# An attention-plus-FFN kernel: weight-block differences moved from GpSimd to VectorE, and a flag set earlier

## The chip, the cores and the metric

The kernel runs on one core of one Trainium2 chip. The metric is the device time of one execution in microseconds (us); every time of a run below is such a time, and the "span" is the somewhat shorter stretch that the profiler covers. The engines of a core are TensorE (PE: matmuls; PEld: its weight loads), VectorE (DVE), ScalarE (ACT), GpSimd (POOL) and SyncE (SP, which here only issues transfers). In the traces below each works through its own queue of instructions in order, and waits where an operand or a buffer is not ready. Tiles lie in one of two memories of the core: PSUM, where every matmul of this kernel writes its result (the pools whose names begin with `ps_`), and SBUF, which holds the rest. Most executions of one kernel agree within about 1%.

## The reference

```python
def _attn_ref(q, k, v):                      # q, k, v: [8, 8, 576, 64] (batch, heads, tokens, 64)
    scores = scale * np.matmul(q, k.transpose(0, 1, 3, 2))
    mask = np.abs(pos[:, None] - pos[None, :]) <= 32          # a window of 32 to each side
    scores = np.where(mask, scores, -1000000000.0)
    ...                                                      # softmax
    return np.matmul(attn, v)

def _moe_ref(x, w_gate, w_val, w_out):       # x: [4608, 512], w_gate, w_val: [512, 1536], w_out: [1536, 512]
    g = x @ w_gate
    silu = g * (1.0 / (1.0 + np.exp(-g)))
    return silu * (x @ w_val) @ w_out
```

## The kernel before

The 4608 tokens go through the FFN in nine chunks of 512. FFN1 of a chunk has twelve blocks. In each, TensorE makes two sums of four matmuls of 128x512 (gate and value) in a PSUM tile `gv`; ScalarE applies SiLU to the first; VectorE multiplies the two into `hT`. The pool `ps_a` holds two such tiles, so block u + 2 can't start before VectorE has finished the product of block u. The attention of later tokens is woven in between.

```python
def ffn1_unit(j, fk):                        # one FFN1 block of chunk j
    gv = ps_a.tile([128, 2, 512], FP32, ...)
    for i, w in enumerate((wg16, wv16)):
        for g in range(GS):                  # GS = 4
            nc.tensor.matmul(out=gv[:, i, :], lhsT=w[:, g, ...], rhs=xts[j][:, g, :], ...)
    nc.scalar.activation(out=ssb, in_=gv[:, 0, :], func=AF.Silu, ...)
    nc.vector.tensor_tensor(out=hts[j][:, fk, :], in0=ssb, in1=gv[:, 1, :], op=ALU.mult)
```

From the second chunk on, FFN2 is computed with seven half-size products in place of eight (Winograd's form of Strassen's scheme). That takes, once, four differences T1 to T4 of blocks of `w_out`, and, for each chunk, four sums S1 to S4 of blocks of `hT`, which VectorE makes during FFN1. GpSimd makes the differences, after it has issued the loads of the third batch:

```python
    turn_x([4, 5, 6], ps_a, cast_act)
    ffn2_sub(0, 3, 0)
    pair_av(7)
    pair_mask(8)                             # VectorE: p = p * mask, 128x1024 f16, both in SBUF
    ffn2_sub(0, 3, 1)
    turn_x([7], ps_a, cast_dve)              # TensorE transposes x, VectorE copies them from PSUM into xT
    load_v(2, range(5))
    wino_weights()
    ...                                      # then FFN1 of the second chunk, which reads xT

def wino_weights():
    ...
    sub = lambda o, a, b: nc.gpsimd.tensor_tensor(out=o, in0=a, in1=b, op=ALU.subtract)
    sub(t3, b22, b12)                        # 128x1536
    sub(wide, b12, b11)                      # wide is f32, the others f16
    cast_pool(t1, wide)
    sub(wide, b22, wide)
    cast_pool(t2, wide)
    sub(t4, b21, wide)
```

At the end a flag says whether all softmax sums were in a safe range (otherwise a general path runs). One small matmul counts the partitions that passed, and VectorE turns the count into the flag. The count lies in `ps_c`, a pool of one buffer, which the first product (`p1`) of the last FFN2 also needs:

```python
def set_flag(good):
    cnt = ps_c.tile([1, 1], FP32, tag="c", name="cnt")
    nc.tensor.matmul(out=cnt, lhsT=good, rhs=ones, ...)
    nc.vector.tensor_scalar(out=flag, in0=cnt, scalar1=127.5, op0=ALU.is_lt, ...)

for j in range(1, NCH):                      # NCH = 9
    ffn1(j)
    if j == NCH - 2:
        good = check_range()                 # five small VectorE instructions
    if j == NCH - 1:
        set_flag(good)
    ffn2(j, ...)                             # p1, p2, p6, p5, p7, p3, p4: 12 matmuls of 128x256 each
```

## Time and profile before

| what | before |
|---|---|
| time, median (first three runs) | 339.58 us (337.96 to 339.7) |
| span of the profiled run | 338.0 us |
| TensorE busy | 316.1 us, 94% |
| wait for xT before the second FFN1 (gap 1) | 5.26 us |
| wait for the flag before the last FFN2 (gap 2) | 2.01 us |

From the page of the kernel before: the span; busy time, share and count of TensorE and VectorE; then two rows in which the span is cut into 40 equal slices, PE with its busy share in tenths and PEclk with the granted TensorE clock in tenths of full speed.

```profile
span 338.0 us, 7194 instructions
...
PE 316.1 (94%) x2888; PEld 183.7 (54%) x2888; DVE 206.9 (61%) x412; ACT 161.9 (48%) x245; POOL 121.9 (36%) x145
...
PE   6789999499999999999999999999999999899791
...
PEclk9999999699999999999999999999999999999987
```

TensorE is the limit. Its row has 9 nearly everywhere, and two dents: a 4 in the eighth slice (59 to 68 us) and a 7 near the end. At the first the clock falls in the same slice, at the second in the slice after it. The view of waits says what TensorE waited for (the columns are total, times, longest):

```profile
PE gv_ps L421 <- DVE xT L265: 5.3, 1, 5.3
...
PE x_ps L504 <- DVE flag L577: 2.0, 1, 2.0
...
PE x_ps L504 <- DVE s_top L476: 0.9, 1, 0.9
```

The timeline shows the first gap. Its columns are the start, the duration, engine, line and operation, out<-in, and in brackets the idle time before. L462 is the subtraction on GpSimd, L316 the mask multiply, L408 the transposes, L265 the xT copy, L421 the FFN1 matmuls.

```profile
56.98 3.12 POOL L462 TENSOR_TENSOR w_top<-wo 128x1536 f16<-128x1536 f16 x1
...
58.10 5.60 DVE L316 TENSOR_TENSOR p_t<-p_t,mask 128x1024 f16<-128x1024 f16 x1
...
58.45 0.39 PE L408 MATMUL xt_ps<-ident,x 128*128 128x128 f16 x4
...
60.03 3.12 POOL L462 TENSOR_TENSOR w_wide<-wo 128x1536 f32<-128x1536 f16 x1
...
63.21 1.82 POOL L268 CAST w_top<-w_wide 128x1536 f16<-128x1536 f32 x1
63.63 0.41 DVE L265 COPY xT<-xt_ps 128x512 f16<-128x512 f16 x1
...
64.10 1.89 PE L421 MATMUL gv_ps<-xT,wg 128*128 128x512 f16 x4 [5.26 <-DVE xT L265]
...
65.78 1.91 PE L421 MATMUL gv_ps<-xT,wv 128*128 128x512 f16 x4
...
67.48 1.31 PE L421 MATMUL gv_ps<-xT,wg 128*128 128x512 f16 x4
```

The xT copy is not slow. It stands in VectorE's queue behind a multiply that took 5.60 us, eight times its usual 0.69, exactly while GpSimd subtracted. After the gap, groups of four matmuls follow each other every 1.7 us instead of every 0.865 us.

The same view at the end of the kernel before. L576 is the count, L428 the last FFN1 product, L577 the flag, L504 the FFN2 products.

```profile
317.55 0.19 PE L576 MATMUL cnt<-ones,good 128*1 128x1 f32 x2
...
318.28 0.69 DVE L428 TENSOR_TENSOR hT<-ssb,gv_ps 128x512 f16<-128x512 f16 x1 [0.24 <-ACT ssb L427]
...
319.56 0.14 DVE L577 TENSOR_SCALAR flag<-cnt 1x1 int32<-1x1 f32 x1
...
319.75 1.91 PE L504 MATMUL x_ps<-wo,hT 128*128 128x256 f16 x12 [2.01 <-DVE flag L577]
...
321.45 2.74 PE L504 MATMUL y_ps<-wo,hT 128*128 128x256 f16 x12
```

The count is done at once, but the flag waits in VectorE's queue for the last FFN1 product and two sums. Meanwhile it holds the PSUM buffer that the first FFN2 product wants.

### The profile page before, as it was taken

How to read it: one execution, taken by the hardware profiler on the slowest of the kernel's cores; microseconds unless marked ns; L12 is line 12 of the kernel's file. 1: busy time of each engine (PE TensorE's matmuls, PEld its weight loads, DVE VectorE, ACT ScalarE, POOL GpSimd, SP SyncE). 2: the span in 40 equal slices, each digit the busy share in tenths (PEclk: the TensorE clock that was granted, in tenths of full speed). 3: DMA queues.
4: the chain of work that ended last, by engine and by line, in shares of the span. 5: the costliest groups of instructions: out<-in, count | busy, mean ns of one | idle time of the engine just before them, and what ended most of it. 6: DMA issues, size and time to landing. Idle time of an engine off the chain costs nothing. (4 is left out here: it accounts for less than half of the span.)

```text
span 338.0 us, 7194 instructions
## 1 busy us (share of the span) xinstructions
PE 316.1 (94%) x2888; PEld 183.7 (54%) x2888; DVE 206.9 (61%) x412; ACT 161.9 (48%) x245; POOL 121.9 (36%) x145
## 2 busy tenths in 40 slices
PE   6789999499999999999999999999999999899791
PEld 3444555144774477447744764486448644754380
DVE  2743375545766786778667767686668556535720
ACT  3864579057753376237533753375337633233220
POOL 8972878993704540356045405360000000000000
PEclk9999999699999999999999999999999999999987
DMA  7999999939949995999999979996531510020003
GB/s 271 171 204 303 216 162 200 152 41 136 114 119 142 156 111 117 121 162 86 192 128 133 118 166 109 151 134 150 109 49 33 142 31 3 31 93 3 0 33 100
DMA packets 154280, 41.31 MB, mean 122 GB/s; under 512 B 137856, under 2 KB 151680, under 8 KB 154240
## 3 DMA queue, kind: packets, MB, share of 16 engines
q0 software_dynamic: 100640, 16.52, 67.5%
q1 hardware_dynamic: 53600, 24.26, 31.5%
q8 instruction: 24, 0.39, 0.5%
q14 instruction: 16, 0.13, 0.1%
HBM read 37.75 MB, written 9.44 MB: 140 GB/s over the span
## 5 line engine op out<-in xcount | busy, mean ns | idle before, releaser
L428 DVE TENSOR_TENSOR hT<-ssb,gv_ps 128x512 f16<-128x512 f16 x108 | 74.3, 688 | 88.9 <-ACT ssb L427 88.9
L427 ACT ACTIVATE ssb<-gv_ps 128x512 f16<-128x512 f32 x108 | 64.5, 597 | 126.2 <-PE gv_ps L421 125.0
L421 PE MATMUL gv_ps<-xT,wg 128*128 128x512 f16 x432 | 112.1, 382 | 5.9 <-DVE xT L265 5.3
L421 PE MATMUL gv_ps<-xT,wv 128*128 128x512 f16 x432 | 111.8, 381 | 0.0
L421 PEld LDWEIGHTS <-wg 128*128 128x128 f16 x432 | 41.7, 98 | 53.8 <-DVE xT L265 5.4
L421 PEld LDWEIGHTS <-wv 128*128 128x128 f16 x432 | 42.5, 98 | 51.6 <-issue 1.1
L223 POOL DMA_DIRECT2D tok<-in_q_dram x30 | 25.4, 848 | 66.1 <-DMA qT<-tok 61.1
L312 ACT ACTIVATE p_t<-s_ps 128x1024 f16<-128x1024 f32 (+1 forms) x40 | 34.7, 924 | 13.1 <-PE s_ps L306 13.1
L504 PEld LDWEIGHTS <-hT 128*128 128x128 f16 x288 | 28.3, 100 | 7.6 <-issue 2.0
L223 POOL DMA_DIRECT2D tok<-in_k_dram x30 | 25.3, 845 | 16.3 <-DMA kT<-tok 12.2
L504 PEld LDWEIGHTS <-s_top 128*128 128x128 f16 x288 | 27.7, 98 | 4.8 <-DVE s_top L476 1.1
L316 DVE TENSOR_TENSOR p_t<-p_t,mask 128x1024 f16<-128x1024 f16 x32 | 25.9, 841 | 1.6 <-ACT p_t L312 0.9
L386 DVE TENSOR_TENSOR x<-o_ps,rall 128x512 f16<-128x512 f32 (+1 forms) x39 | 25.4, 650 | 1.3
L504 PE MATMUL x_ps<-w_top,s_top 128*128 128x256 f16 x192 | 23.8, 273 | 0.9 <-DVE s_top L476 0.9
L242 POOL DMA_DIRECT2D v<-in_v_dram x24 | 21.4, 904 | 0.4 <-DMA tok<-in_q_dram 0.4
L476 DVE TENSOR_TENSOR s_top<-hT 128x768 f16<-128x768 f16 (+2 forms) x48 | 20.1, 418 | 0.0
L265 DVE COPY v<-v 64x512 f16<-64x512 f16 x46 | 14.8, 321 | 1.6
L688 ACT ACT_TABLE_LOAD x12 | 15.4, 1283 | 0.2
L532 DVE TENSOR_TENSOR osb<-y_ps,kept 128x512 f32<-128x512 f32 (+1 forms) x16 | 10.5, 655 | 7.8 <-ACT p_t L312 4.0
L368 PEld LDWEIGHTS <-p_t 128*64 128x64 f16 x576 | 10.7, 110 | 6.9 <-issue 5.1
L262 ACT ACTIVATE kept<-x_ps 128x512 f32<-128x512 f32 (+1 forms) x18 | 9.4, 532 | 10.4 <-PE x_ps L504 10.4
L504 PE MATMUL x_ps<-wo,hT 128*128 128x256 f16 x96 | 12.2, 279 | 2.0 <-DVE flag L577 2.0
(81 smaller groups left out, 276.6 us busy)
## 6 DMA issues: line engine op xcount, KB each, us to landing
out_dram<-osb SPq DMA_DIRECT2D x32, 256.0 KB, 2.5
v<-in_v_dram POOLq DMA_DIRECT2D x24, 128.0 KB, 4.8
tok<-in_q_dram POOLq DMA_DIRECT2D x24, 128.0 KB, 4.7
tok<-in_k_dram POOLq DMA_DIRECT2D x24, 128.0 KB, 5.3
qk_st<-in_q_dram SPq DMA_DIRECT2D x4, 576.0 KB, 7.2
qk_st<-in_k_dram SPq DMA_DIRECT2D x4, 576.0 KB, 9.0
v<-in_v_dram POOLq DMA_DIRECT2D x16, 96.0 KB, 5.3
wo<-in_moe_w_out_dram POOLq DMA_DIRECT2D x4, 384.0 KB, 21.4
```

Of the source, the lines that this page charges most:

```text
L223: nc.gpsimd.dma_start(out=t[0:n].rearrange("p (h d) -> p h d", d=D), in_=src[b].rearrange("h s d -> s h d")[128 * m:128 * m + n])
L242: nc.gpsimd.dma_start(out=dst[:, 2 * m, :, 0:D], in_=src[128 * m - 32:128 * m + 96])
L265: nc.vector.tensor_copy(out=o, in_=i)
L312: nc.scalar.activation(out=o, in_=s, func=AF.Exp, bias=0.0, scale=1.0 / float(D) ** 0.5)
L316: nc.vector.tensor_tensor(out=flat, in0=flat, in1=mask, op=ALU.mult)
L386: nc.vector.tensor_tensor(out=x16s[m][:, a], in0=ov[:, :, :, 0:D], in1=r.unsqueeze(3).to_broadcast([128, a.stop - a.start, 4, D]), op=ALU. ...
L421: nc.tensor.matmul(out=gv[:, i, :], lhsT=w[:, g, 128 * fk:128 * fk + 128], rhs=xts[j][:, g, :], start=(g == 0), stop=(g == GS - 1))
L427: nc.scalar.activation(out=ssb, in_=gv[:, 0, :], func=AF.Silu, bias=0.0, scale=1.0)
L428: nc.vector.tensor_tensor(out=hts[j][:, fk, :], in0=ssb, in1=gv[:, 1, :], op=ALU.mult)
L476: tt = lambda o, a, b, op: nc.vector.tensor_tensor(out=o, in0=a, in1=b, op=op)
L504: nc.tensor.matmul(out=dst[n], lhsT=lhs[:, f, 128 * n:128 * n + 128], rhs=rhs[:, f, :], start=(first and f == 0 and (split or n == 0)), st ...
L688: nc.scalar.activation(out=dummy, in_=rall[0:1, 0, 0:1], func=func, bias=0.0, scale=1.0)
```

## The change

The intent is to take the weight differences off GpSimd, where they are slow, and to spread them in eight pieces over VectorE's idle time in the second FFN1. The second part sets the flag inside the last FFN1, where nobody waits for its buffer.

```diff
 def wino_weights():
-        wide = qkst.tile([128, FKS // 2, 256], FP32, tag="qkst", name="w_wide")
 ...
-        sub = lambda o, a, b: nc.gpsimd.tensor_tensor(out=o, in0=a, in1=b, op=ALU.subtract)
-        sub(t3, b22, b12)
-        sub(wide, b12, b11)
-        cast_pool(t1, wide)
-        sub(wide, b22, wide)
-        cast_pool(t2, wide)
-        sub(t4, b21, wide)
+        return [lambda o=o[:, f:f + 3], a=a[:, f:f + 3], b=b[:, f:f + 3]:
+                nc.vector.tensor_tensor(out=o, in0=a, in1=b, op=ALU.subtract)
+                for o, a, b in ((t3, b22, b12), (t1, b12, b11), (t2, b22, t1), (t4, b21, t2))
+                for f in (0, 3)]
 ...
-    wino_weights()
+    tw = wino_weights()
 ...                                          # in ffn1(j), after block u
+            if j == 1:
+                for f in {0: tw[0:1], 1: tw[1:3], 3: tw[3:5], 4: tw[5:7], 5: tw[7:8]}.get(u, ()):
+                    f()
+            if j == NCH - 1 and u == 4:
+                set_flag(good)
 ...
-        if j == NCH - 1:
-            set_flag(good)
```

## The prediction

> **What bounds the kernel now.** TensorE. The page has PE busy 94% of the span of 338.0 us (VectorE 61%, ScalarE 48%, GpSimd 36%). So the change is worth what it removes from TensorE's gaps. The timeline shows two large ones, and the change aims at both.
>
> **Gap 1, before the second FFN1 (58.84 to 64.10 us).** The view of waits has one wait of 5.26 us of PE gv_ps for VectorE's xT copy. That copy took 0.41 us, but stood behind one mask multiply (128x1024 f16, both inputs in SBUF) that took 5.60 us, against 0.69 us for its neighbours. It ran from 58.10 to 63.70, while GpSimd ran two subtractions of weight blocks back to back (56.98 to 60.10, 60.03 to 63.15). The Trainium skill, "SBUF — State Buffer", section "Who interferes with whom", says that a VectorE instruction with two SBUF inputs contends with a GpSimd instruction that reads SBUF and blocks; the trace agrees (5.60 against 0.69 us, ending 0.55 us after the second subtraction). After the gap the first FFN1 matmuls ran at half rate: the first three groups of four took 1.68, 1.70 and 1.14 us from start to start instead of 0.865 (granted clock 0.69 in that stretch).
>
> Without the GpSimd work (15.9 us, 56.98 to 72.8) the multiply should take 0.69 us and the xT copy start when its transposes end (58.84), so the matmuls start at about 59.4: 4.7 us gained. A gap of 0.5 us should not lower the clock: another 1.9 us.
>
> **Gap 2, before the last FFN2 (317.6 to 319.75 us).** 2.0 us of PE x_ps waiting for the flag (0.14 us on VectorE, in order behind the last FFN1 product, which ends at 318.97, and two sums). The first FFN2 product doesn't need the last FFN1 block; it waited only because the flag's count holds its PSUM buffer. With the flag at the fifth block it starts at once: 2.0 us gained. The 24 matmuls after the gap took 1.91 + 2.54 us instead of 1.31 each (granted clock 0.85): 1.8 us gained if TensorE does not pause. The second product needs the last block just when it starts: perhaps 0.1 us of wait.
>
> **What is added.** Eight f16 subtractions of 128x768 on VectorE, in the second FFN1. The sums of that shape take 0.55 us (0.47 from start to start): 4 us in all. VectorE there has 0.8 to 1.3 us idle before each FFN1 product; two pieces and a product need 1.55 us of the 1.73 us per block. I expect 0 to 0.4 us of TensorE gaps. GpSimd issues the next q, k loads some 10 us earlier; no TensorE wait for a load shows, so that gains nothing.
>
> **Sum.** 4.7 + 1.9 + 2.0 + 1.8 - 0.2 = about 10.2 us, all on TensorE's chain, which is full between the gaps, so little should be given back. 339.6 - 10.2 = 329.4 us. Range 327.5 to 332. Faster by over 2%: 0.93; within 2%: 0.06; slower: 0.01.
>
> **What would show it.** No mask multiply over 0.8 us near 58 us; gv_ps waiting about 0.5 us for xT; full-rate matmuls from the first of the second FFN1; pieces of 0.55 us; no PE wait for the flag; last FFN2 in 7 x 1.31 us.
>
> **What would make it wrong.** Clock lowered all the same, by phase or load rather than by gaps (up to 3.7 us lost); the pieces holding back FFN1 products, so that PSUM buffers come free late; earlier loads delaying transposes that FFN1 or attention need; a new wait in the last FFN2, where sums were ready early only because TensorE stood still.

## The result, and the profile after

The changed kernel takes 329.42 us (median of 4 runs, 328.64 to 330.21) against 339.64 us before. The ratio is 0.9704, 95% interval 0.9668 to 0.974: faster. Ratios below are the mean time of one kernel's fast executions over that of the other's in the same rounds, without the execution that was profiled, so they are not quite the ratio of the medians quoted. The result is correct.

From the page of the changed kernel, the same lines:

```profile
span 326.6 us, 7197 instructions
...
PE 312.4 (96%) x2888; PEld 182.3 (56%) x2888; DVE 205.9 (63%) x420; ACT 161.8 (50%) x245; POOL 106.1 (33%) x139
...
PE   6789999999999999999999999999999999899992
...
PEclk9999999999999999999999999999999999999998
```

Both dents are gone, and the clock row has no dip left before the tail. (The 8 that stays in the PE row is the wait of 0.9 us for sums, which e9_tighter below takes up.) VectorE's busy time even fell by 1.0 us, although it took on eight instructions: the time in which the multiply was blocked had been counted as busy.

The timeline of the changed kernel at gap 1 (L462 is now the piece on VectorE):

```profile
57.84 0.68 DVE L316 TENSOR_TENSOR p_t<-p_t,mask 128x1024 f16<-128x1024 f16 x1
58.18 0.39 PE L408 MATMUL xt_ps<-ident,x 128*128 128x128 f16 x4
...
58.61 0.42 DVE L265 COPY xT<-xt_ps 128x512 f16<-128x512 f16 x1
...
59.09 1.04 PE L421 MATMUL gv_ps<-xT,wg 128*128 128x512 f16 x4 [0.52 <-DVE xT L265]
...
59.97 1.03 PE L421 MATMUL gv_ps<-xT,wv 128*128 128x512 f16 x4
...
62.26 0.55 DVE L462 TENSOR_TENSOR w_top<-wo 128x768 f16<-128x768 f16 x1
...
63.99 1.02 DVE L462 TENSOR_TENSOR w_top<-wo 128x768 f16<-128x768 f16 x2
```

The multiply takes 0.68 us, TensorE waits 0.52 us, and the matmuls run at full rate from the first. Two pieces take 1.02 us and fit between two FFN1 products.

The timeline of the changed kernel at gap 2 (the count is now L572, the FFN2 products L500):

```profile
298.67 0.19 PE L572 MATMUL cnt<-ones,good 128*1 128x1 f32 x2
...
310.88 1.47 PE L500 MATMUL x_ps<-wo,hT 128*128 128x256 f16 x12
...
311.71 0.69 DVE L428 TENSOR_TENSOR hT<-ssb,gv_ps 128x512 f16<-128x512 f16 x1 [0.24 <-ACT ssb L427]
312.19 1.47 PE L500 MATMUL y_ps<-wo,hT 128*128 128x256 f16 x12
...
313.50 1.47 PE L500 MATMUL x_ps<-w_top,s_top 128*128 128x256 f16 x12
```

There is no idle time in brackets any more, and the products follow each other every 1.31 us.

For the bookkeeping, one stage measure serves for all runs below: from the end of the transposes for xT (start plus duration of that L408 line) to the first FFN2 matmul of that chunk. It was 87.33 - 58.84 = 28.49 us before and is 80.39 - 58.57 = 21.82 us after: 6.67 us gained. At the end, from the start of the last group of FFN1 matmuls to the start of the last FFN2 product, it was 329.27 - 316.59 = 12.68 us and is 318.75 - 310.02 = 8.73 us: 3.95 us gained. Against this, the stretch between the two measures is 0.37 us longer (229.63 us against 229.26), of which 0.12 us is the count, now paid inside FFN1; the other 0.25 us was not traced, and in the profiles of e1 and e2 that stretch is longer still (229.96 and 229.81 us). The rest of the profiles' 11.4 us of difference in span is scatter at both ends. The stretch before the transposes was 0.27 us shorter in this execution, and the tail after ScalarE's last copies started was 6.35 us against 7.22 (in a second profile of the changed kernel it is 6.7).

### The profile page after: what moved, and what is told of

Its sections match the earlier page's. It is cut to its first block, busy times and chain, and to the rows that moved or that the text cites. A ratio compares the mean times of both kernels' runs of the same rounds, so it can differ in the third digit from the quotient of the medians.

```text
span 326.6 us, 7197 instructions
## 1 busy us (share of the span) xinstructions
PE 312.4 (96%) x2888; PEld 182.3 (56%) x2888; DVE 205.9 (63%) x420; ACT 161.8 (50%) x245; POOL 106.1 (33%) x139
## 5 line engine op out<-in xcount | busy, mean ns | idle before, releaser
L421 PE MATMUL gv_ps<-xT,wg 128*128 128x512 f16 x432 | 110.9, 379 | 1.2 <-ACT xT L262 0.7
L500 PEld LDWEIGHTS <-hT 128*128 128x128 f16 x288 | 27.6, 98 | 5.1
L500 PEld LDWEIGHTS <-s_top 128*128 128x128 f16 x288 | 27.6, 98 | 4.7 <-DVE s_top L472 1.1
L500 PE MATMUL x_ps<-w_top,s_top 128*128 128x256 f16 x192 | 23.8, 273 | 0.9 <-DVE s_top L472 0.9
L316 DVE TENSOR_TENSOR p_t<-p_t,mask 128x1024 f16<-128x1024 f16 x32 | 20.8, 686 | 1.4 <-ACT p_t L312 0.8
L368 PE MATMUL o_ps<-v,p_t 128*64 128x66 f16 x576 | 12.8, 196 | 1.1 <-DVE p_t L352 1.1
```

Source lines behind the costliest of these rows:

```text
L316: nc.vector.tensor_tensor(out=flat, in0=flat, in1=mask, op=ALU.mult)
L368: nc.tensor.matmul(out=o[h // 4][64 * i:64 * i + 64, 66 * (h % 4):66 * (h % 4) + 66], lhsT=p[:, place(b, h)[0], i, place(b, h)[1], :], rhs ...
L421: nc.tensor.matmul(out=gv[:, i, :], lhsT=w[:, g, 128 * fk:128 * fk + 128], rhs=xts[j][:, g, :], start=(g == 0), stop=(g == GS - 1))
L500: nc.tensor.matmul(out=dst[n], lhsT=lhs[:, f, 128 * n:128 * n + 128], rhs=rhs[:, f, :], start=(first and f == 0 and (split or n == 0)), st ...
```

## The experiments

Eleven kernels ran. The theory: GpSimd's subtractions read SBUF and thereby block the mask multiply, which has both inputs in SBUF; TensorE's pause that follows also lowers its clock. Rivals are named with each run.

### Each part alone

e1_flag_only is the kernel before with only the flag moved; e2_weights_only is the changed kernel with the flag put back.

```diff
# e1_flag_only, against before
+            if j == NCH - 1 and u == 4:
+                set_flag(good)
...
-        if j == NCH - 1:
-            set_flag(good)
# e2_weights_only, against the changed kernel: the same lines the other way round
```

> The kernel before with only the flag moved into the last FFN1. If the two parts of the change are independent and gap 2 costs its 2.0 us of wait plus 1.8 us at a lowered clock: 3.7 to 3.9 us faster than before (ratio about 0.989), gap 1 unchanged at about 5.3 us. Rival, that gap 2 was hidden by the output DMA at the end or comes back as a wait for the sums: 0 to 2 us faster (ratio 0.994 to 1).

> The changed kernel with the flag put back after the last FFN1. If independent: 6.3 to 6.8 us faster than before (ratio about 0.981), gap 2 unchanged at 2.0 us with two slow products after it. Rival, that the gain of gap 1 is partly given back by the VectorE pieces or by loads issued earlier: under 5.5 us.

Measured: e1_flag_only 335.61 us against 339.44 (ratio 0.9884, interval 0.985 to 0.9919), so about 3.9 us, with the wait of gap 1 still there (5.31 us). e2_weights_only 334.43 us (ratio 0.9832, 0.9781 to 0.9883), about 5.7 us, a little under what was expected. Its stage measure is 21.81 us, the same as with the whole change, so the gain of gap 1 is not given back. The profile shows one thing that blurs the total: in this execution the very first FFN1, at 21 us, long before anything that was changed, lost about 1.7 us at half rate. Of the other profiles only e8_lump's shows that. The two parts add up to 9.6 us, against 10.0 us together (1 - 0.9704 of 339.6): they are independent within the scatter.

### Is it a lock, and on what?

e4_mask_late keeps GpSimd's work and only swaps two instructions on VectorE.

```diff
-    pair_mask(8)
     ffn2_sub(0, 3, 1)
     turn_x([7], ps_a, cast_dve)
+    pair_mask(8)
```

> The kernel before, GpSimd work kept, but the mask multiply of the eighth pair is issued on VectorE after the xT copy instead of ahead of it. Theory, GpSimd's reads block a VectorE instruction with two SBUF inputs and nothing else: the xT copy (PSUM source) still takes 0.41 us and FFN1 starts at about 59.4; the multiply still lasts till about 63.7, so the first FFN1 product comes at 63.7 instead of 61.7 and TensorE waits about 1.6 us for a PSUM buffer two blocks later, without a drop of the clock: 4 to 5 us faster than before. Rival A, VectorE as a whole is slow while GpSimd works: the copy is slow too and little is gained. Rival B, the multiply was slow for a reason of its own at that place (data or PSUM), not for GpSimd: it takes 0.69 us here and all 6.6 us are gained.

The timeline of e4_mask_late:

```profile
58.53 0.42 DVE L265 COPY xT<-xt_ps 128x512 f16<-128x512 f16 x1 [0.68 <-PE xt_ps L408]
58.87 4.47 DVE L316 TENSOR_TENSOR p_t<-p_t,mask 128x1024 f16<-128x1024 f16 x1
...
63.26 1.27 DVE L428 TENSOR_TENSOR hT<-ssb,gv_ps 128x512 f16<-128x512 f16 x2
...
63.99 1.02 PE L421 MATMUL gv_ps<-xT,wg 128*128 128x512 f16 x4 [1.35 <-DVE hT L428]
```

The copy, whose source is PSUM, takes its usual 0.42 us although GpSimd is subtracting (56.61 to 62.78 in this run), so rival A falls. The multiply is blocked again, for 4.47 us, at another place, so rival B falls. The FFN1 products, with one input in SBUF and one in PSUM, keep their 0.69 us while GpSimd goes on working. TensorE waits 1.35 us for a PSUM buffer, and its clock doesn't drop. The time is 333.56 us (ratio 0.9839, 0.9798 to 0.988), about 5.5 us faster, somewhat more than the 4 to 5 expected; the stage measure is 23.32 us, 5.17 us gained. A swap of two lines brings most of what moving all the work brings at gap 1.

e6_pool_writes keeps GpSimd busy but lets it only write. Its output is wrong, which doesn't matter for the time.

```diff
-        sub(t3, b22, b12)   ...and the other subtractions and casts
+        for t in (t3, wide, t1, t2, t4, wide, t3, wide, t1, t2, t4, wide):
+            nc.gpsimd.memset(t, 0.0)
```

> The kernel before with GpSimd's subtractions and casts replaced by twelve memsets that only write (results wrong on purpose: the differences are zero). If it is GpSimd's SBUF reads that block the mask multiply: it takes 0.69 us though GpSimd is busy beside it, and gap 1 goes, 6.3 to 6.8 us faster than before. Rival, any GpSimd access to SBUF blocks it: the multiply stays as long as the memsets that it meets, and gap 1 stays in part or whole.

The timeline of e6_pool_writes:

```profile
57.79 1.42 POOL L463 MEMSET w_wide<- 128x1536 f32 x1
57.96 0.68 DVE L316 TENSOR_TENSOR p_t<-p_t,mask 128x1024 f16<-128x1024 f16 x1
...
59.11 2.74 POOL L463 MEMSET w_top<- 128x1536 f16 x2
```

The multiply lies wholly inside a stretch of memsets without a pause and takes 0.68 us. The stage measure is 21.81 us, the same as with the change: 6.68 us gained. That points to GpSimd's reading. A memset is also another kind of instruction than a subtraction, but the traces hold a third kind: near 13 us, in all thirteen profiles, GpSimd copies two pieces of `v` from SBUF to SBUF while VectorE does mask multiplies of the same shape. From the kernel before (L352 is a multiply, L268 a copy):

```profile
12.98 0.61 POOL L268 COPY v<-v 64x512 f16<-64x512 f16 x1
13.19 0.94 DVE L352 TENSOR_TENSOR p_t<-p_t,mask 128x1024 f16<-128x1024 f16 x1
13.64 0.97 POOL L268 COPY v<-v 64x512 f16<-64x512 f16 x1
14.06 1.09 DVE L352 TENSOR_TENSOR p_t<-p_t,mask 128x1024 f16<-128x1024 f16 x1
```

The multiplies take 0.94 and 1.09 us instead of 0.69 (the slower one 1.09 to 1.10 us in every profile), and the second copy, which meets the first multiply, 0.97 us instead of 0.61. So two kinds that read SBUF, subtraction and copy, block, and the one that only writes does not. The whole time was 332.12 us against 340.06 (ratio 0.9757, 0.97 to 0.9813), nominally 8.3 us; the expected 6.3 to 6.8 lie at the edge of that interval, and in that batch the kernel before scattered from 338.57 to 341.89.

### How long does the lock hold?

In the kernel before the multiply arrived during one subtraction and waited through the next one too. e5_pool_pieces cuts GpSimd's work into eight pieces, back to back.

```diff
-        sub(t3, b22, b12)   ...and the other subtractions and casts
+        for o, a, b in ((t3, b22, b12), (t1, b12, b11), (t2, b22, t1), (t4, b21, t2)):
+            for f in (0, 3):
+                nc.gpsimd.tensor_tensor(out=o[:, f:f + 3], in0=a[:, f:f + 3],
+                                        in1=b[:, f:f + 3], op=ALU.subtract)
```

> The kernel before with the differences still on GpSimd, but as eight f16 subtractions of 128x768 back to back (about 1.6 us each, 12.5 us in all). If the lock goes back at the end of each GpSimd instruction, the mask multiply waits for at most one piece: it lasts at most 2.3 us, and 3 to 6 us are gained. If back-to-back GpSimd instructions keep VectorE out (the multiply of before waited through two of them), it lasts till GpSimd pauses, up to 12 us, and the kernel is 3 to 7 us slower than before.

The timeline of e5_pool_pieces:

```profile
56.36 6.44 POOL L464 TENSOR_TENSOR w_top<-wo 128x768 f16<-128x768 f16 x4
...
57.81 11.88 DVE L316 TENSOR_TENSOR p_t<-p_t,mask 128x1024 f16<-128x1024 f16 x1
...
62.73 3.23 POOL L464 TENSOR_TENSOR w_top<-wo,w_top 128x768 f16<-128x768 f16 x2
65.91 3.21 POOL L464 TENSOR_TENSOR ws_rest<-wo,w_top 128x768 f16<-128x768 f16 x2
```

Less GpSimd work in smaller pieces made it worse. The multiply lasted 11.88 us: through the rest of the first piece and all seven others, to 0.57 us after the last one ended. The kernel took 347.64 us (ratio 1.0258). So the end of an instruction alone does not let the waiting VectorE in. The pieces' own time per piece is 1.59 us from start to start ((62.73 - 56.36) / 4). The Trainium skill, "Perfetto Trace Analysis", section "GPSIMD Engine Instruction", advises to time GpSimd so and not by the reported spans; here the two agree (6.44 / 4 = 1.61).

What lets VectorE in? In the kernel before it came in just where GpSimd's cast had to wait for the subtraction ahead of it, whose result it read; that cast then took 1.82 us, the other one 1.46. e10_pool_chain has the same eight pieces, in an order in which a piece often has to wait for the one just ahead.

```diff
+        three = [(t1, b12, b11), (t2, b22, t1), (t4, b21, t2)]
+        for f, (o, a, b) in ([(0, x) for x in three] + [(3, x) for x in three]
+                             + [(0, (t3, b22, b12)), (3, (t3, b22, b12))]):
+            nc.gpsimd.tensor_tensor(...)      # pieces as above
```

> The GpSimd pieces of 128x768 as in the run with pieces, same number and size, but in an order in which the second and third each read what the one just ahead wrote, so that GpSimd pauses between them. There the mask multiply waited 11.2 us through seven pieces that followed each other without a pause; in the kernel before it came in where a cast had to wait for the subtraction ahead. If VectorE comes in at GpSimd's first pause: the multiply lasts at most 2.3 us, gap 1 is at most 2.2 us, 4.5 to 6.6 us faster than before. Rival, subtraction after subtraction keeps VectorE out, pause or not (in the kernel before it was the cast, another kind of instruction, that let it in): the multiply lasts 5 us or more, no gain or slower.

The timeline of e10_pool_chain:

```profile
57.71 1.65 POOL L465 TENSOR_TENSOR w_top<-wo 128x768 f16<-128x768 f16 x1
57.99 1.93 DVE L316 TENSOR_TENSOR p_t<-p_t,mask 128x1024 f16<-128x1024 f16 x1
...
59.44 1.97 POOL L465 TENSOR_TENSOR w_top<-wo,w_top 128x768 f16<-128x768 f16 x1
...
60.31 1.04 PE L421 MATMUL gv_ps<-xT,wg 128*128 128x512 f16 x4 [1.59 <-DVE xT L265]
```

Order alone cuts the multiply from 11.88 to 1.93 us. The first piece ends at 59.36; the second starts 0.08 us later, and in that pause VectorE comes in. Now the second piece pays, with 1.97 us instead of 1.64. That the pause is what lets VectorE in fits every case on record, but each order of GpSimd's work was run once; between the two copies near 13 us, which don't read each other's results, there is also a pause (0.05 us), and VectorE came in there too. The kernel took 333.68 us (ratio 0.9832, 0.9787 to 0.9877), about 5.7 us faster than before with all the work still on GpSimd; the stage measure is 22.88 us.

### Does a pause of TensorE lower its clock?

e3_fill_gap1 and e7_fill_gap2 put matmuls that nobody reads into the two gaps of the kernel before.

```diff
# e3_fill_gap1
     turn_x([7], ps_a, cast_dve)
+    idle_mms(23)
# e7_fill_gap2
             set_flag(good)
+            idle_mms(9)
```

> The kernel before with 23 matmuls of 128x512 that nobody reads put on TensorE where it waits 5.3 us for the xT copy. If the half rate after gap 1 comes from TensorE standing still: FFN1 still starts at about 64.1 but at full rate from its first matmul, 1.9 us faster than before. Rival, the clock drops there by phase or load, whatever TensorE does: no gain, still half rate.

> The kernel before with 9 matmuls of 128x512 that nobody reads in gap 2. If the slow products after gap 2 come from TensorE standing still 2 us: the last FFN2 takes 7 x 1.31 us, 1.8 us faster than before, the wait for the flag itself stays. Rival, clock by phase or load: no gain.

The timeline of TensorE in e3_fill_gap1 (L557 is the filling):

```profile
58.57 5.13 PE L557 MATMUL warm<-mask 128*128 128x512 f16 x23
63.73 1.04 PE L421 MATMUL gv_ps<-xT,wg 128*128 128x512 f16 x4
```

The multiply was still blocked (5.33 us), but the FFN1 matmuls ran at full rate at once. The stage measure is 26.29 us against 28.49. Of the 2.2 us, 1.93 come after the gap: from the first FFN1 matmul to FFN2 it is 85.03 - 63.73 = 21.30 us against 23.23. In e7_fill_gap2 the first two FFN2 products came 1.31 us apart each, instead of 1.70 and 2.56, 1.64 us gained. One profile each would be thin, but the other profiles agree: the second FFN1 started at half rate in all four with a pause of 5.3 us or more before it, and in none of the nine with a shorter one or a filled gap; the last FFN2 started at full rate in all six without a pause in gap 2 (after, e1, e8, e9, e11 and the filled e7). So the half rate came from TensorE standing still. The times of the whole kernels can't show it: the medians of the fast executions, 337.47 us (ratio 0.9926, 0.9825 to 1.0027) and 338.12 us (0.9948, 0.9872 to 1.0024) against 340.06, are inconclusive.

The profiles also add a limit to this. Seven of them have gap 2 unfilled, 2.0 us each time. The clock was lowered after it in five (before, e2, e3, e5, e6) and not in two (e4, e10). From the TensorE timeline of e10_pool_chain:

```profile
314.41 1.47 PE L502 MATMUL x_ps<-wo,hT 128*128 128x256 f16 x12 [2.02 <-DVE flag L575]
```

These 12 matmuls took 1.47 us, not 1.91, after the same pause. Single pauses before or in the second FFN1 of 1.59 (e10), 1.35 (e4) and 1.82 us (e8, next) did not lower it; the 5.3 us of gap 1 where it stayed empty (before, e1, e7) and the 11.5 us of e5 always did. The Trainium skill, "TensorE: Matmul & The Clock Gate", section "What's actually happening", says that the array runs at full or at half rate, judged over free-running windows of 3.4 us. That agrees with half rate here, and with a 2 us pause that costs something in some executions only; the windows themselves no run here shows. The half rate in the first FFN1 of e2 and e8 doesn't follow from one pause: there TensorE had several of 0.2 to 1.1 us close together, in every profile, and two of thirteen were slowed. What decides there was not tested.

### Does the spreading matter?

e8_lump is the changed kernel with all eight pieces after one block.

```diff
-                for f in {0: tw[0:1], 1: tw[1:3], 3: tw[3:5], 4: tw[5:7], 5: tw[7:8]}.get(u, ()):
+                for f in {1: tw}.get(u, ()):
```

> The changed kernel with all eight VectorE pieces after the second FFN1 block instead of spread over five blocks. If what matters is how long one FFN1 product is held up: the lump of 3.8 us delays the third product by about 2.7 us beyond its slack, TensorE waits about 2 us for a PSUM buffer, and the kernel is 1.5 to 2.5 us slower than the changed one (7.5 to 8.5 us faster than before, against 10 us). Rival, VectorE has spare time on average, so the place is indifferent: as fast as the changed kernel.

The view of waits of e8_lump has a line that the changed kernel has not:

```profile
PE gv_ps L421 <- DVE hT L428: 1.8, 1, 1.8
```

The time was 331.48 us (ratio 0.9734 to before), 2.1 us over the changed kernel by medians of different rounds, but only 1.0 us by the two ratios, whose intervals overlap. So the whole time doesn't settle it; the stage does: 23.79 us against 21.82, so 1.97 us lost, of which 1.8 us are the wait above. The same eight instructions cost TensorE no wait when spread and 2 us in one lump. VectorE's spare time comes in portions: in the kernel before it sat idle for 0.7 to 1.3 us before each of the second to sixth products of the second FFN1.

### What was left

e9_tighter takes away two more waits of TensorE that the changed kernel's profile lists. e11_changed_again is the changed kernel, in the same rounds.

```diff
     turn_x([7], ps_a, cast_dve)
+    pair_av(8, ps_c, False)                  # and no longer after the third block of the second FFN1
...
-        if j == NCH - 2:
-            good = check_range()
...
+            if j == NCH - 1 and u == 2:
+                good = check_range()
             if j == NCH - 1 and u == 4:
                 set_flag(good)
```

> The changed kernel once more, to stand beside the next one in the same rounds. 329.4 us and a ratio to the kernel before of about 0.970, as when it was first measured.

> The changed kernel with two more TensorE gaps taken away: the range check moved from between the last FFN1 but one and its FFN2 (where its 1.8 us on VectorE hold up the sums: 0.86 us of TensorE wait) into the third block of the last FFN1; and the attention product of the eighth pair moved from the third block of the second FFN1 into the 0.52 us in which TensorE waits for the xT copy. If TensorE's chain is full everywhere else: 0.86 + 0.45 = 1.3 us faster than the changed kernel. Rival, the next wait takes their place: no difference.

Measured in the same rounds: before 339.53 us, e11_changed_again 329.70 us (ratio 0.9708), e9_tighter 328.36 us (ratio 0.967, 0.9637 to 0.9703). The difference of 1.3 us is what was expected; the intervals overlap, but each of the six executions of e9_tighter is faster than each of the six of e11_changed_again. The wait for the sums (0.86 us) is gone from its view of waits. The attention product now runs from 58.55 to 59.00, in the gap, and FFN1 starts at 59.07, as without it. So it beats both kernels.

## Why the prediction was right

- **TensorE is the limit and its two gaps are the whole gain.** Right. 6.67 and 3.95 us were gained in the two stages, and of that only 0.37 us was lost again in the stretch between. The predicted time was 329.4 us, the measured one 329.42; that it is this close is luck, as one kernel's executions scatter by 1.6 us.
- **Gap 1: a blocked multiply, 4.7 us.** Right: the wait fell from 5.26 to 0.52 us. e4 and e10 show that it was GpSimd's work beside it, and that this work needn't have left GpSimd; e6 and the copies near 13 us show that it was the reading. The prediction said only that the instruction blocks. It didn't ask for how long; e5 and e10 show that the block outlasts one instruction and ended where GpSimd paused.
- **The clock after gap 1, 1.9 us.** Right. FFN1 with its attention product took 21.30 us instead of 23.23, and e3 shows 1.93 us by filling the gap alone.
- **Gap 2: 2.0 us of wait and 1.8 us of clock.** Right in sum: about 3.9 us in e1. The 1.8 us were read from one profile in which the pause did lower the clock; in two of seven it didn't. Such a term should be given as a chance.
- **0.1 us of wait for the second product.** None was seen. The first of its matmuls that reads the last block is the sixth: by estimate from the 1.31 us of its twelve it starts at about 312.7 us, after the last FFN1 product has ended at 312.40.
- **The pieces: 0 to 0.4 us.** None was seen. FFN1 ran without a wait, each piece took 0.55 us, and e8 shows that the same pieces in a lump cost 1.97 us.
- **GpSimd issues loads 10 us earlier.** It issued the next one at 65.12 instead of 72.76 us, 7.6 us earlier, because it then waited 7.47 us for a buffer to come free. It was off the chain, as said.

## What to carry to other kernels

When an instruction takes several times what its neighbours of the same shape take, look at what GpSimd did at that moment, before you blame the engine or its queue: here one blocked multiply of 0.69 us cost TensorE 6.7 us, and an order of instructions, on either engine, cured most of it. Work moved onto a queue that feeds the limiting engine must be cut into portions that fit the idle time between the instructions waited for; the average share of busy time doesn't tell. Value a pause of TensorE by more than its length, as what follows may run at half rate; but ask several profiles, because a pause of 2 us does so only sometimes.

## What the Trainium skill lacked or had wrong

- "SBUF — State Buffer", section "SBUF: two separate sides", has it that, of GpSimd and a VectorE instruction with two SBUF inputs, the one that starts first gets the shared ports "for the whole instruction" and the other blocks, unless GpSimd only writes. The trace agrees on who blocks whom: two SBUF inputs against GpSimd's reads 5.60 us instead of 0.69, against GpSimd's writes 0.68 us, and a PSUM source 0.42 us. On how long the measurement differs: VectorE waited not for one instruction of GpSimd but through all that followed without a pause, 11.88 us through the end of one piece and seven more of 1.6 us. It came in at the first pause of about 0.1 us (1.93 us in e10).
- The same page lacks how the block appears in a profile: here as busy time of VectorE. The 32 mask multiplies of this shape are listed with 25.9 us busy before (mean 841 ns) and 20.8 us after (686 ns).
- "TensorE: Matmul & The Clock Gate", section "Why this matters for your kernels", asks for no pauses over about 3 us. Here single pauses of 2.0 us lowered the clock in 5 of 7 profiles; three of 1.35 to 1.82 us, one profile each, did not. So 3 us is not a safe length in this kernel.
